# First two halves' plain output tiles moved ahead of both pairs; half of the third half's transposes given to transfers

## Chip, cores and metric

The kernel runs on one core of one Trainium2 chip. Its time is the device time of one execution in microseconds (us); before the change the median of four runs is 237.45 us (237.02 to 237.99). The engines are named as the profile names them: PE multiplies matrices, DVE, ACT and POOL work element by element, SP only issues transfers. POOL issues transfers too (the profile's software queue; SP's are the hardware queue).

## What is computed

Attention over 4 batches of 8 heads, 768 positions of 64 values, followed by a gated feed-forward network. A query sees the first 8 keys and the last 96:

```python
scores = scale * np.matmul(q, k.transpose(0, 1, 3, 2))
keep = is_global | is_local
scores = np.where(keep, scores + bias, -1000000000.0)
a = softmax(scores)
x = np.matmul(a, v)          # then (B, H, S, D) -> (B*S, H*D) = (3072, 512)
out = (np.maximum(x @ w_gate, 0.0) * (x @ w_val)) @ w_out   # 512 -> 1536 -> 512
```

Inputs and result are float32; the chip multiplies in 16-bit types.

## The kernel before

**Tiling.** The 3072 rows are eight halves (half a sequence, 384 rows each), numbered 0 to 7; the code writes s for a half in attention and c in the network. A half has four pairs of heads p = 0 to 3 in attention, and three tiles of 128 rows in the output stage.

**Attention of a half.** Keys and queries are loaded as float32 (`load_qk`, L113) and cast to 16 bits. They must then be transposed so that the head dimension lies over the partitions. Halves 0 and 1 do it on PE. Half 2 does so too: `cast` (L826, two POOL casts a pair), then `T2_piece` (L982), which makes six PE transposes of 128x128 (`piece_t`, L299), three DVE copies that put the keys into order (`piece_copy_k`, L278 to L280) and one ACT copy of the queries (L985). Halves 3 to 7 use `early_pieces` (L378): POOL casts (`piece_cast2`, L367), six transposing transfers from SP (`piece_x`, L372), and three POOL copies a pair that put the keys into order (`piece_order`, L276, which shows as L278 to L284). Then `attention_pieces` (L543) makes scores (L515), ACT exponentials (L524), DVE masks (L536), the product with the values (`piece_av`, L431), and the division (ACT L440 and L446, DVE L453).

**Values.** `load_v_half` (L162) loads the first eight rows of a batch (POOL L141) and spreads them to the other key tiles with six small copies from SP (L146), which wait for that load; then it loads the rest (POOL L154).

**Network of a half.** For each of twelve blocks of hidden columns a gate product and a value product of four matmuls each (`products`, L748). ACT makes the rectified gate (L757), DVE multiplies it with the value product into `ht` (L764). All of these go through three PSUM banks, `ff_ps`: a product can start only when an earlier bank's reader is done. Weights come in three groups of four blocks, `wg` and `wv` 0 to 2 (L173), cast in flight on POOL's queue.

**Output stage.** A plain tile (`single`, L791) is four parts of three 512-column matmuls (L781), an ACT copy (L786) and a store from SP (L787). Two tiles together (`Pair`, L605) take seven products of half-size blocks rather than eight (L634), with sums of `ht` blocks made by DVE beforehand (`sums`, L627 to L630), sums of weights made once (`weight_sums`, L600), and additions afterwards (L647). Halves 0 and 1 have one plain tile and one pair each; later halves pair up their third tiles too.

**Order.** Every engine runs its instructions in the order in which they are written. The head of the kernel is written out by hand (L838 to L981). From there `weave` (L813) interleaves: a list of network items sets the pace, each with the same weight, and attention pieces are placed at fractions of that list. The first weave (L988) has 20 items, the second (L994) 38: the last blocks of halves 0 and 1, and then their output stages, while attention of half 2 and the preparation of half 3 go in between. `F0[8]` to `F0[11]` are gate 4, value 4, gate 5 and value 5 of half 0.

Of the kernel before, what the change touches and what calls it, by code (L numbers as in the profile page):

```python
# [10 lines left out]
FP16 = mybir.dt.float16  # L11
# [5 lines left out]
def kernel(  # L17
# [12 lines left out]
    nc = tc.nc  # L30

    B, H, S, D = q.shape
# [6 lines left out]
    HP = H // 2  # L39
    QH = S // 2  # L40
    NN = 3
# [13 lines left out]
    for half in range(2):  # L55
# [32 lines left out]
    qTb = [const.tile([128, HP, 2, QH], BF16, name=f"qT{i}") for i in range(2)]  # L88
    kNb = [const.tile([128, HP, QH], BF16, name=f"kN{i}") for i in range(2)]

    qT2 = [qTb[1].rearrange("d p e t -> d (p e t)")[:, i * HP * QH : (i + 1) * HP * QH].rearrange(
        "d (p t) -> d p t", p=HP) for i in range(2)]
    qc = [const.tile([128, NN, DM], BF16, name=f"qc{i}") for i in range(2)]
    kc = [const.tile([128, NN, DM], BF16, name=f"kc{i}") for i in range(2)]
# [11 lines left out]
    def w_of(t, dc, fc):  # L106
        f = fc % GW
        return t[fc // GW][:, dc, f * 128 : (f + 1) * 128]


    qs_of, ks_of = {}, {}

    def load_qk(s, h0, h1, eng=nc.sync):  # L113
        b, half = divmod(s, 2)
        if s not in qs_of:
            qs_of[s] = stage.tile([128, H, NN * D], FP32, name="qs")
            ks_of[s] = stage.tile([128, H, NN * D], FP32, name="ks")
        for src, dst in ((k, ks_of[s]), (q, qs_of[s])):
            eng.dma_start(
                out=dst[:, h0:h1, :],  # L120
                in_=src[b, h0:h1, half * QH : (half + 1) * QH, :].rearrange(
                    "h (p n) d -> p h (n d)", n=NN))
# [17 lines left out]
    def load_v_globals(b):  # L140
        nc.gpsimd.dma_start(out=v_dst(b, 0, NG, 0),  # L141
                            in_=v[b, :, 0:NG, :].rearrange("h p d -> p h d"))
# [19 lines left out]
    def load_v_half(s):  # L162
        b, half = divmod(s, 2)
        if half == 0:
            load_v_globals(b)
            spread_v_globals(b)
        for j in range(4) if half == 0 else range(4, NT):
            load_v(b, j)
# [4 lines left out]
    def load_w_group(i):  # L173
        load_w(wg[i], moe_w_gate, i * GW * 128, (i + 1) * GW * 128)
        load_w(wv[i], moe_w_val, i * GW * 128, (i + 1) * GW * 128)
# [190 lines left out]
    def piece_cast2(s, p, dst, src):  # L366
        nc.gpsimd.tensor_copy(  # L367
            dst[s % 2].rearrange("t n (h d) -> t h n d", d=D)[:, 2 * p : 2 * p + 2],
            src[s][:, 2 * p : 2 * p + 2, :].rearrange("t e (n d) -> t e n d", n=NN))

    def piece_x(dst, src, n):
        nc.sync.dma_start_transpose(out=dst[:, :, n * 128 : (n + 1) * 128], in_=src[:, n])  # L372

    def piece_order(s, p):
        b, half = divmod(s, 2)
        put_keys(nc.gpsimd.tensor_copy, nc.gpsimd.tensor_copy, kT[b % 2][p], kNb[s % 2][:, p], half)
# [209 lines left out]
    NP = N_FC // 2  # L586
# [151 lines left out]
    def ffn_pieces(c):  # L738
        ht_of[c] = ht = ht_pool.tile([128, N_FC, QH], FP16, name="ht")
        st = {}  # L740
        pair = Pair((c, 0), (c, 1))
        first = {}

        def products(key, w, fc, d0, d1):
            if d0 == 0:
                st[key] = ff_psum.tile([128, 512], FP32, name="ff_ps")
            for dc in range(d0, d1):
                nc.tensor.matmul(st[key][:, 0:QH], lhsT=w_of(w, dc, fc), rhs=xT_of[c][:, dc, :],  # L748
                                 start=(dc == 0), stop=(dc == N_DC - 1))
            return st[key]  # L750

        def gate(fc, d0=0, d1=N_DC):
            psg = products(f"g{fc % 4}", wg, fc, d0, d1)
            if d1 < N_DC:
                return
            gr = gr_pool.tile([128, QH], BF16, name="grelu")
            nc.scalar.activation(gr, psg[:, 0:QH], AF.Relu, bias=0.0, scale=1.0)  # L757
            st["r", fc] = gr

        def val(fc, d0=0, d1=N_DC):  # L760
            psv = products("v", wv, fc, d0, d1)
            if d1 < N_DC:
                return
            nc.vector.tensor_tensor(ht[:, fc, :], psv[:, 0:QH], st["r", fc], op=ALU.mult)  # L764

            if c > 1 and 7 <= fc < N_FC - 1:
                if fc == 7:
                    first[0] = pair.sums(0, 4)
                first[0][fc - 7]()

        f1 = []
        for fc in range(N_FC):
            f1.append((0.65, lambda *d, fc=fc: gate(fc, *d)))
            f1.append((0.65, lambda *d, fc=fc: val(fc, *d)))

        def outp(n, part, after):
            if part == 0:
                st["o"] = ff_psum.tile([128, DM], FP32, name="ff_ps")
            ps2 = st["o"]
            for fc in range(part * NP // 2, (part + 1) * NP // 2):  # L780
                nc.tensor.matmul(ps2, lhsT=ht[:, fc, n * 128 : (n + 1) * 128], rhs=wo_sb[:, fc, :],  # L781
                                 start=(fc == 0), stop=(fc == N_FC - 1))
            if part == 3:
                osb = obuf[:, n_results[0] % 2, 0:2]
                n_results[0] += 1
                nc.scalar.copy(osb, ps2)  # L786
                nc.sync.dma_start(out=out_v[c, n], in_=osb)  # L787
            for f in after:
                f()

        def single(n, *after):  # L791
            after = after or ((),) * 4
            return [(0.65, lambda part=part: outp(n, part, after[part])) for part in range(4)]

        late = pair.sums(0 if c < 2 else 4, NP)
        if c < 2:
            return f1, single(2, *([f] for f in late)) + pair.items()
        if c % 2 == 0:
            return f1, pair.items({"1": late[0:2], "2": late[2:4]}, fresh=True)

        space = qTb[0].rearrange("d p e t -> d (p e t)").bitcast(FP16)
        across = Pair((c - 1, 2), (c, 2), space.rearrange("t (s c z) -> t s c z", s=4, c=NP))
        sums = across.sums(0, NP)
        return f1, (pair.items({"1": late[0:2], "2": late[2:4], "4": sums[0:1], "6": sums[1:2], "5": sums[2:4]}, fresh=True)
                    + across.items(split=c == NHALF - 1))


    def spread(items, first, last, n=None):

        n = n or len(items)  # L810
        return [(first + (i + 0.5) / n * (last - first), f) for i, (_, f) in enumerate(items)]

    def weave(f_items, *placed):  # L813
        total = sum(t for t, _ in f_items)
        a_items = sorted((x for p in placed for x in p), key=lambda x: x[0])
        done, ai = 0.0, 0
        for t, f in f_items:
            f()
            done += t
            while ai < len(a_items) and a_items[ai][0] * total <= done:  # L820
                a_items[ai][1]()
                ai += 1
        for _, f in a_items[ai:]:
            f()
# [3 lines left out]
        piece_cast(s, p, 0, eq)  # L828

    V, P, A = nc.vector, nc.gpsimd, nc.scalar  # L830
    f1_0, f2_0 = ffn_pieces(0)
    f1_1, f2_1 = ffn_pieces(1)
    G = [slice(2 * GW * i, 2 * GW * (i + 1)) for i in range(N_FC // GW)]
    F0 = [f for _, f in f1_0]
    LAST = N_DC - 1
# [85 lines left out]
    piece_biased(1, 0)  # L921
    load_v(0, 3, 24)
    load_w_group(1)
    load_w_group(2)
    load_qk(2, 0, H, nc.gpsimd)
    load_w(wo_sb, moe_w_out, 0, DM)
    for f in gate[0:3]:
        f(0, LAST)
# [35 lines left out]
    piece_inverse_wide(1, 2)  # L964
    piece_ln_wide(1, 3)
    piece_mul_wide(1, 2)
    F0[9]()
    piece_inverse_wide(1, 3)
    piece_mul_wide(1, 3)
    F0[10]()  # L970
    F0[11]()
    for p in range(HP):
        nc.gpsimd.memset(kT[1][p][:, 3, 32:128].bitcast(mybir.dt.uint32), 0)
# [1 line left out]
    nc.gpsimd.memset(vbuf[1][:, NT - 1, :].bitcast(mybir.dt.uint32), 0)  # L975
    for j in range(NT):
        fill_ones(nc.gpsimd, 1, j)
    for p in range(HP):
        cast(2, p, P, P)
    load_v_half(2)  # L980

    def T2_piece(p):  # L982
        piece_t(2, p, *QKB, apart=True)
        piece_copy_k(2, p)
        nc.scalar.copy(qT2[0][:, p], tp_of[2, p, 0])  # L985

    T2 = [(0.0, lambda p=p: T2_piece(p)) for p in range(HP)]
    weave(f1_1[G[0]] + f1_0[G[1]][4:] + f1_1[G[1]],  # L988
          [(0.05 + 0.06 * j, lambda j=j: fill_ones(nc.vector, 0, j)) for j in range(NT)],
          [(0.1 + 0.2 * i, lambda h=h: setup_mask(h)) for i, h in enumerate((0, 1, 6, 7))],  # L990
          [(0.6, lambda: load_qk(3, 0, H)), (0.6, lambda: load_v_half(3))],
          spread(T2, 0.55, 0.95))
    sums_wo = [(0.0, f) for i in (0, 3) for f in weight_sums(i, i + 3)]
    weave(f1_0[G[2]] + f1_1[G[2]] + f2_0 + f2_1,  # L994
          spread(attention_pieces(2), 0.02, 0.86, 30), spread(early_pieces(3), 0.1, 0.76),
          spread(sums_wo, 0.08, 0.4))

    for c in range(2, NHALF):
        placed = []
# [6 lines left out]
        f1, f2 = ffn_pieces(c)  # L1006
# [36 lines left out]
```

The softmax here doesn't subtract the row's maximum and nothing guards it: scores larger than these inputs give would overflow.

## Time and profile before

| what | value |
|---|---|
| median of four runs | 237.45 us |
| the profiled execution: its time | 237.38 us |
| its span, first to last instruction | 235.6 us |
| outside the span | 1.8 us |
| PE busy | 97% of the span |
| DVE, ACT, POOL busy | 79%, 62%, 38% |
| granted TensorE clock | 0.999 |
| read from and written to memory | 28.38 and 6.29 MB |

The chain of work that ended last lies 79% on PE, 7% on POOL, 6% on DVE and 4% on transfers. A row of a timeline gives start, duration, engine, line, operation, what is written and read, and a count; square brackets give the idle time of the engine before it and what ended it. PE durations overlap: what a group costs is the distance from its start to the start of the next. In `ff_ps<-xT,wg` the tile left of the arrow is written.

### The profile page before, as it was taken

The page shows a single profiled execution, that of the slowest core. Times are in us where ns is not written, and L with a number is a line of the kernel's source. Part 1 is how long each engine was busy: PE and PEld are TensorE (multiplying, and loading weights), DVE is VectorE, ACT ScalarE, POOL GpSimd, SP SyncE. Part 2 cuts the span into 40 slices and gives each one's busy share as a digit, 9 for nine tenths or more (in the row PEclk, how much of TensorE's full clock was granted, in tenths as well). Part 3 has the DMA queues.
Part 4 walks back from the last instruction along what each step waited for, and adds up shares of the span by engine and source line. Part 5 has one row for each costly group of instructions (what it writes and reads, how often), then busy time and mean ns, then how long its engine had stood idle before and what let it go on. Part 6 is the DMA issues. An engine that isn't in the chain of part 4 may idle for free.

```text
span 235.6 us, 5509 instructions
## 1 busy us (share of the span) xinstructions
PE 229.2 (97%) x2021; PEld 158.2 (67%) x2021; DVE 186.5 (79%) x466; ACT 146.0 (62%) x321; POOL 89.0 (38%) x191
## 2 busy tenths in 40 slices
PE   8889999999999999999999999999999999999994
PEld 4675756655778666856688666856679566865683
DVE  6878767779988779786999789886899779773784
ACT  7999855677624887467742887567842687524300
POOL 8998904933492066406580066306230000000000
PEclk9999999999999999999999999999999999999999
DMA  6999999998369856856497854857512200020005
GB/s 169 207 174 182 205 273 271 173 108 266 70 168 163 266 145 95 52 180 201 90 81 120 253 159 90 53 151 228 91 24 89 92 0 3 0 92 0 1 3 178
DMA packets 71419, 30.43 MB, mean 129 GB/s; under 512 B 47744, under 2 KB 70784, under 8 KB 71392
## 3 DMA queue, kind: packets, MB, share of 16 engines
q0 software_dynamic: 34896, 10.27, 38.8%
q1 hardware_dynamic: 36496, 19.82, 30.1%
q8 instruction: 16, 0.26, 0.4%
q14 instruction: 11, 0.09, 0.1%
HBM read 28.38 MB, written 6.29 MB: 147 GB/s over the span
## 4 chain that ended last, share of the span: by engine, by line
PE 79%; POOL 7%; DVE 6%; DMA 4%; issue 2%; ACT 1%; POOLq 0%; DVEq 0%
PE ff_ps L748 46%; PE ff_ps L634 20%; PE av_ps L431 6%; DMA wv<-in_moe_w_val_dram 4%; POOL vbuf L154 3%; PE ff_ps L781 2%; PE av_ps L515 2%; PE qk_ps L515 1%; DVE ht L764 1%; POOL kc L131 1%; DVE wo_sum L600 1%; DVE obuf L647 1%; DVE es L536 1%; POOL wg L171 1%; ACT es L524 1%
## 5 line engine op out<-in xcount | busy, mean ns | idle before, releaser
L757 ACT ACTIVATE grelu<-ff_ps 128x384 bf16<-128x384 f32 x96 | 46.7, 489 | 52.1 <-PE ff_ps L748 39.0
L748 PE MATMUL ff_ps<-xT,wv 128*128 128x384 bf16 x384 | 78.0, 327 | 0.2 <-DMA wv<-in_moe_w_val_dram 0.2
L748 PE MATMUL ff_ps<-xT,wg 128*128 128x384 bf16 x384 | 77.8, 326 | 0.0
L764 DVE TENSOR_TENSOR ht<-ff_ps,grelu 128x384 f16<-128x384 f32 x96 | 53.4, 557 | 27.2 <-PE ff_ps L748 22.9
L748 PEld LDWEIGHTS <-wv 128*128 128x128 bf16 x384 | 36.0, 98 | 24.2 <-issue 1.3
L748 PEld LDWEIGHTS <-wg 128*128 128x128 bf16 x384 | 36.4, 97 | 21.2 <-issue 0.5
L647 DVE TENSOR_TENSOR obuf<-ff_ps,obuf 128x512 f32<-128x512 f32 (+1 forms) x46 | 27.6, 604 | 5.3 <-ACT rcp L446 2.2
L367 POOL CAST kc<-ks 128x384 bf16<-128x384 f32 x20 | 10.6, 569 | 54.0 <-DMA ks<-in_k_dram 54.0
L453 DVE TENSOR_TENSOR xT<-av_ps,rcp 64x384 bf16<-64x384 f32 x48 | 26.5, 552 | 5.1 <-ACT rcp L446 4.3
L536 DVE TENSOR_TENSOR es<-es,m_all 128x432 bf16<-128x432 bf16 (+3 forms) x108 | 30.3, 326 | 0.2 <-ACT es L524 0.2
L440 ACT ACTIVATE lnd<-av_ps 64x384 f32<-64x384 f32 x48 | 23.3, 485 | 11.1 <-PE av_ps L431 10.3
L524 ACT ACTIVATE es<-qk_ps 128x432 bf16<-128x432 f32 (+2 forms) x54 | 27.7, 532 | 0.0
L154 POOL DMA_DIRECT2D vbuf<-in_v_dram x29 | 24.7, 861 | 0.1
L431 PE MATMUL av_ps<-es,vbuf 128*128 128x216 bf16 (+4 forms) x216 | 21.4, 226 | 0.0
L431 PEld LDWEIGHTS <-vbuf 128*128 128x128 bf16 x216 | 18.2, 98 | 4.8 <-DVE xT L453 0.4
L634 PEld LDWEIGHTS <-ht 128*128 128x128 f16 x198 | 18.6, 97 | 3.4 <-DVE ht L764 0.5
L634 PEld LDWEIGHTS <-hsum 128*128 128x128 f16 x192 | 18.5, 98 | 2.1
L634 PE MATMUL ff_ps<-wo_sb,ht 128*128 128x256 f16 x132 | 18.5, 272 | 0.2 <-DVE ht L764 0.2
L634 PE MATMUL ff_ps<-wo_sum,hsum 128*128 128x256 f16 x144 | 17.2, 273 | 0.0
L446 ACT ACTIVATE rcp<-lnd 128x384 f32<-128x384 f32 x24 | 12.6, 524 | 0.7
L524 ACT ACTIVATE es<-av_ps 128x432 bf16<-128x432 f32 (+2 forms) x18 | 9.5, 528 | 2.0 <-PE qk_ps L515 2.0
L515 PEld LDWEIGHTS <-kT 64*128 64x128 bf16 x216 | 6.6, 94 | 6.1 <-issue 3.8
(130 smaller groups left out, 264.2 us busy)
## 6 DMA issues: line engine op xcount, KB each, us to landing
out_dram<-obuf SPq DMA_DIRECT2D x22, 256.0 KB
ks<-in_k_dram SPq DMA_DIRECT2D x5, 768.0 KB
qs<-in_q_dram SPq DMA_DIRECT2D x5, 768.0 KB
vbuf<-in_v_dram POOLq DMA_DIRECT2D x23, 120.0 KB, 4.6
wv<-in_moe_w_val_dram POOLq DMA_DIRECT2D x3, 512.0 KB, 9.8
wo_sb<-in_moe_w_out_dram POOLq DMA_DIRECT2D x1, 1536.0 KB, 21.1
wg<-in_moe_w_gate_dram POOLq DMA_DIRECT2D x2, 512.0 KB, 9.8
ks<-in_k_dram SPq DMA_DIRECT2D x4, 192.0 KB
```

The source lines that it names most:

```text
L154: nc.gpsimd.dma_start(out=v_dst(b, NG + r0, NG + r0 + n, j), in_=v[b, :, KT * j + r0 : KT * j + r0 + n, :].rearrange("h p d -> p h d"))
L431: nc.tensor.matmul(av3[:, :, a : a + w], lhsT=vb[:, j, z0 : z0 + 128], rhs=es[:, c : c + NN * w].rearrange("k (n p) -> k n p", n=NN), star ...
L440: nc.scalar.activation(ln[o0 : o0 + 64], av[d0 : d0 + 64, 0:QH], AF.Ln, bias=0.0, scale=1.0)
L453: nc.vector.tensor_tensor(xT_of[s][r, p, :], av_of[s, p, e][r, 0:QH], av_of[s, p, "r"][r], op=ALU.mult)
L515: nc.tensor.matmul(banks[e][:, c : c + NN * w], lhsT=kT[b % 2][p][r, j, :], rhs=q3[:, :, a : a + w], start=True, stop=True)
L524: nc.scalar.activation(es[:, 0:cols], ps[:, 0:cols], AF.Exp, bias=0.0, scale=scale)
L536: nc.vector.tensor_mul(e4, e4, mk)
L634: nc.tensor.matmul(ps[:, c0 : c0 + DH], lhsT=lhs(i), rhs=rhs(i), start=(i == 0), stop=(i == NP - 1), skip_group_check=True)
L647: add = lambda o, x, y: nc.vector.tensor_tensor(o, x, y, op=ALU.add)
L748: nc.tensor.matmul(st[key][:, 0:QH], lhsT=w_of(w, dc, fc), rhs=xT_of[c][:, dc, :], start=(dc == 0), stop=(dc == N_DC - 1))
L757: nc.scalar.activation(gr, psg[:, 0:QH], AF.Relu, bias=0.0, scale=1.0)
L764: nc.vector.tensor_tensor(ht[:, fc, :], psv[:, 0:QH], st["r", fc], op=ALU.mult)
```

## The change

Seven edits:

1. Pairs 2 and 3 of half 2 go the way of halves 3 to 7: POOL casts, six transfers that transpose 128x256 blocks (a new first pair `p` in `piece_x`), six POOL copies for the keys. Pairs 0 and 1 stay on PE; their casts come after those of pairs 2 and 3, and they are placed at 0.65 to 0.95 of the first weave.
2. Keys and queries of half 2 are loaded ahead of the third group of weights, not behind it.
3. Gate 5 of half 0 goes ahead of value 4.
4. The first weave takes the rest of half 0's second group ahead of half 1's first group.
5. The output stages of halves 0 and 1 run as plain tile, plain tile, pair, pair (before: plain tile, pair, plain tile, pair).
6. The pair of half 0 keeps its sums in the query buffer of half 0, which is free by then. Its sums are placed behind the parts of half 1's plain tile, and those of half 1's pair between products of half 0's pair.
7. The sums of weights are spread over 0.1 to 0.4 of the second weave (before: 0.08 to 0.4).

```diff
-    def piece_x(dst, src, n):
-        nc.sync.dma_start_transpose(out=dst[:, :, n * 128 : (n + 1) * 128], in_=src[:, n])
+    def piece_x(dst, src, n, p=0):
+        nc.sync.dma_start_transpose(out=dst[:, p:, n * 128 : (n + 1) * 128], in_=src[:, n, 128 * p :])
...
+        space = qTb[0].rearrange("d p e t -> d (p e t)").bitcast(FP16).rearrange("t (s c z) -> t s c z", s=4, c=NP)
+        if c == 0:
+            pair = Pair((c, 0), (c, 1), space)
         late = pair.sums(0 if c < 2 else 4, NP)
-        if c < 2:
-            return f1, single(2, *([f] for f in late)) + pair.items()
+        if c == 0:
+            return f1, single(2), late, pair
+        if c == 1:
+            return f1, single(2, *([f] for f in pair_0[0])), pair_0[1].items(
+                {"1": late[0:1], "2": late[1:2], "4": late[2:3], "6": late[3:4]}) + pair.items()
...
     load_w_group(1)
+    load_qk(2, 0, H, nc.gpsimd)
     load_w_group(2)
-    load_qk(2, 0, H, nc.gpsimd)
...
-    F0[9]()
+    F0[10]()
     piece_inverse_wide(1, 3)
     piece_mul_wide(1, 3)
-    F0[10]()
+    F0[9]()
     F0[11]()
...
-    for p in range(HP):
+    for to, src in ((kc, ks_of), (qc, qs_of)):
+        for p in (2, 3):
+            piece_cast2(2, p, to, src)
+        for n in range(NN):
+            piece_x((kNb if to is kc else qT2)[0], to[0], n, 2)
+    for p in (0, 1):
         cast(2, p, P, P)
     load_v_half(2)
+    for p in (2, 3):
+        piece_order(2, p)
...
-    T2 = [(0.0, lambda p=p: T2_piece(p)) for p in range(HP)]
-    weave(f1_1[G[0]] + f1_0[G[1]][4:] + f1_1[G[1]],
+    T2 = [(0.0, lambda p=p: T2_piece(p)) for p in range(2)]
+    weave(f1_0[G[1]][4:] + f1_1[G[0]] + f1_1[G[1]],
...
-          spread(T2, 0.55, 0.95))
+          spread(T2, 0.65, 0.95))
...
-    weave(f1_0[G[2]] + f1_1[G[2]] + f2_0 + f2_1,
+    weave(f1_0[G[2]] + f1_1[G[2]] + single_0 + single_1 + pairs_01,
...
-          spread(sums_wo, 0.08, 0.4))
+          spread(sums_wo, 0.1, 0.4))
```

More of the change, by code (lines that the diff above doesn't have):

```diff
@@ L793, in single @@
             return [(0.65, lambda part=part: outp(n, part, after[part])) for part in range(4)]
+        space = qTb[0].rearrange("d p e t -> d (p e t)").bitcast(FP16).rearrange("t (s c z) -> t s c z", s=4, c=NP)
+        if c == 0:
+            pair = Pair((c, 0), (c, 1), space)
         late = pair.sums(0 if c < 2 else 4, NP)
-        if c < 2:
-            return f1, single(2, *([f] for f in late)) + pair.items()
+        if c == 0:
[3 more added lines that the diff above has]
+                {"1": late[0:1], "2": late[1:2], "4": late[2:3], "6": late[3:4]}) + pair.items()
         if c % 2 == 0:
             return f1, pair.items({"1": late[0:2], "2": late[2:4]}, fresh=True)
-        space = qTb[0].rearrange("d p e t -> d (p e t)").bitcast(FP16)
-        across = Pair((c - 1, 2), (c, 2), space.rearrange("t (s c z) -> t s c z", s=4, c=NP))
+        across = Pair((c - 1, 2), (c, 2), space)
         sums = across.sums(0, NP)
@@ L830 @@
     V, P, A = nc.vector, nc.gpsimd, nc.scalar
-    f1_0, f2_0 = ffn_pieces(0)
-    f1_1, f2_1 = ffn_pieces(1)
+    f1_0, single_0, *pair_0 = ffn_pieces(0)
+    f1_1, single_1, pairs_01 = ffn_pieces(1)
     G = [slice(2 * GW * i, 2 * GW * (i + 1)) for i in range(N_FC // GW)]
```

## The prediction, made before the change was run

> **What bounds the kernel now.** First the page's busy times and slices:
>
> ```profile
> PE 229.2 (97%) x2021; PEld 158.2 (67%) x2021; DVE 186.5 (79%) x466; ACT 146.0 (62%) x321; POOL 89.0 (38%) x191
> PE   8889999999999999999999999999999999999994
> ```
>
> PE is the only engine that is nearly always busy, and in every slice but the ends. A high share can hide stalls, so next I read PE's own waits, all of them:
>
> ```profile
> PE ff_ps L249 <- DVE obuf L187: 1.0, 1, 1.0
> PE qk_ps L329 <- ACT lnd L485: 0.6, 1, 0.6
> PE av_ps L299 <- ACT obuf L263: 0.4, 1, 0.4
> PE ff_ps L344 <- DVE qT L315: 0.2, 1, 0.2
> PE ff_ps L748 <- DMA wv<-in_moe_w_val_dram: 0.2, 1, 0.2
> PE ff_ps L634 <- DVE ht L764: 0.2, 1, 0.2
> PE av_ps L515 <- DVE xT L453: 0.2, 1, 0.2
> ```
>
> The columns are total, times and longest. The first four lie in the first 17 us, which the change leaves alone. Only two of the rest (DMA wv, DVE xT) lie where it acts. So time is won only by taking work off PE or ending these two waits, and lost only where PE gets a new wait. PE's timeline, the DVE's and POOL's and SP's, and the transfer shares by window, say how near such waits are.
>
> **1. Pairs 2 and 3 of half 2 by transfers.** PE's timeline around the transposes:
>
> ```profile
> 39.95 0.50 PE L299 MATMUL qk_ps<-ident,obuf 128*128 128x128 bf16 x6
> 40.28 0.81 PE L748 MATMUL ff_ps<-xT,wg 128*128 128x384 bf16 x4
> 40.93 0.81 PE L748 MATMUL ff_ps<-xT,wv 128*128 128x384 bf16 x4
> 41.58 0.50 PE L299 MATMUL qk_ps<-ident,obuf 128*128 128x128 bf16 x6
> 41.92 0.81 PE L748 MATMUL ff_ps<-xT,wg 128*128 128x384 bf16 x4
> ```
>
> Six transposes take 0.33 to 0.34 us from start to next start, with no gap on either side. Two pairs go: 2 x 0.335 = **-0.67 us**. The Trainium skill says more: "TensorE: Matmul & The Clock Gate", Part 4 (PE-mode transpose), puts a 128x128 transpose in a kernel's context at about 275 ns. Twelve would be 3.3 us and the result 234.1 us. The row's own mean is 219 ns, near that figure, but the six start 56 ns apart: the figure is the length of one, not what it holds PE for. I take the row.
>
> Also removed: six DVE copies of keys (per pair 0.52 + 0.17 + 0.2 to 0.4, 2 us in all) and two ACT copies of 0.48. PE waited for neither between 30.2 and 58.9, so they count nothing; neither backlog reaches the second weave (DVE waits for PE 0.74 us at 48.06).
>
> Added: the four casts on POOL replace four of the same size. Six key copies on POOL, at half 4's rows 0.53 + 0.2 to 0.48 + 0.22 to 0.47 each pair, make 2 to 3 us. SP issues six transfers at most as long as half 3's 1.2 to 2.0 us, under 9 us on a queue that idles from 4.8 to 46.9. Queued behind them are SP's six spreads of values (L146) and the loads for half 3.
>
> The keys' timing: POOL now waits for half 2's keys and queries:
>
> ```profile
> 37.21 0.50 POOL L263 CAST obuf<-ks 128x384 bf16<-128x384 f32 x1 [7.50 <-DMA ks<-in_k_dram]
> 39.18 0.51 POOL L263 CAST obuf<-qs 128x384 bf16<-128x384 f32 x1 [1.47 <-DMA qs<-in_q_dram]
> ```
>
> The load of queries took 2.0 us behind that of keys, and wv of group 1 landed at 30.14. Loaded next, keys land near 32.1 and queries near 34.1. Casts and transfers follow; with both slowed twofold the ordered keys are there by 45. Pair 2 is first scored at 51.7: cost zero, cover 6 us. The third weights slip from about 35 to 39; first used at 46.5: zero. The output weights keep their place in the queue.
>
> What is not covered so well is the transfers' share. Half 3's six full-size transposes took, by share times window, 0.47 x 1.25, 0.52 x 1.25, 0.41 x 2.0, 0.57 x 1.1, 0.42 x 1.4 and 0.57 x 1.0, about 0.6 us each (one window holds part of a store). Half-size ones: 0.3 each, 1.8 us, laid among casting loads that keep the share at 1.2. No row shows the two kinds side by side. From below, the overlap in that share swallows them: 0. From above, each small packet costs twice: 3.6 us. "DMA: Bandwidth & Descriptors", section on queues, rings and completion order, says that each engine takes turns between queues by packet, which speaks against the change, since 256-byte-row transposes get turns beside the weights; but it loses the loads no more than the transposes' own time. By the rule 1.8 us, by the worst reading 3.6; I take 1.8 as the upper part of what is likely. It delays the output weights (landed 46.7, DVE wants them at 50.7), the values and the spreads behind them. These were all down by 51.5 (the share falls from 2.28 at 50.5 to 0.35 at 51.5). Their reader, L431, starts at 54.14, or 53.5 with PE 0.64 ahead by then (items 1 and 2): cover 2.0 us, and 0.2 more because the last key tile is read fourth. Cost taken as zero, but only just: 0 to +1.4.
>
> **2. Gate 5 ahead of value 4.** PE's timeline:
>
> ```profile
> 29.53 0.48 PE L468 MATMUL qk_ps<-kN,vbuf 128*64 128x72 bf16 x10
> 30.19 0.82 PE L748 MATMUL ff_ps<-xT,wv 128*128 128x384 bf16 x4 [0.18 <-DMA wv<-in_moe_w_val_dram]
> ```
>
> Groups of L468 lie 0.31 apart, and a change to L748 costs 0.1 (26.11 to 26.52). Without the wait the next group starts at 29.94: 0.25 us is lost here (the 0.18 is counted from a modelled end). Gate 5 has its weights, and value 4 then starts at 30.6, behind the landing at 30.14: **-0.25**.
>
> It buys a new wait. ACT now makes gate 5's relu (0.85 after the gate's start: 30.79) ahead of pair 3's inverse, which starts at 31.19 and ends at 31.71 (before: 30.57 to 31.09). DVE multiplies pair 3's xT at 31.74 and value 4's ht behind it, 32.21 to 32.77. Two values now stand side by side (value 4, value 5, gate 6, value 6), so value 6, due at 32.54, finds all three banks held: by ht 4 until 32.77, gate 6 until 33.23, value 5 until 33.24. With 0.05 for the signal it starts at 32.82: **+0.28**. From below 0, if a bank comes free sooner; from above +0.75, if it is given gate 6's bank. I take ht 4's, whose reader ends first. Half 1's gates start 2.6 us later than before in the order, so xT's delay of half a us costs nothing.
>
> **3. The sums of weights from 0.1.** DVE's timeline:
>
> ```profile
> 56.93 0.68 DVE L536 TENSOR_TENSOR es<-es,m_all 128x432 bf16<-128x432 bf16 x1
> 57.54 0.85 DVE L600 TENSOR_TENSOR wo_sum<-wo_sb,wo_sum 128x768 f16<-128x768 f16 x1
> 58.31 1.13 DVE L453 TENSOR_TENSOR xT<-av_ps,rcp 64x384 bf16<-64x384 f32 x2
> ```
>
> DVE is full from 50.4, and PE's next scores (L515) wait for the first xT. The products before end at 57.94 + 0.65, plus 0.09 for the change of form: 58.68; scores started at 58.91, 0.23 late. The seventh sum stands at 0.08 + 6.5/8 x 0.32 = 0.340 of the list, xT at 0.02 + 11.5/30 x 0.84 = 0.342: just behind. Now the sum is at 0.344, behind xT, which is freed of 0.55 to 0.85 us: **-0.23**. Late next is ht of block 10, which the two plain tiles do not want before 61.
>
> **4. Output order, sums elsewhere, first weave's order.** PE from 59.36 to 75.36 is 8 plain parts x 0.65 + 14 products x 0.655 + 6 value groups x 0.275 = 16.0: no idle time to win. The same instructions run on PE, DVE, ACT and SP in another order: 0. Two risks. Half 1's plain tile needs block 11's ht (61.0) by its last part, at about 63.3: covered. Two pairs back to back hand over banks without a plain tile between; half 3's pair and the pair across follow each other in 118.41 to 128.66 without a PE wait, so 0, bound 0 to +0.5. The first store precedes half 3's query transposes on SP, the second follows them, and its buffer is reused 2 us later than it lands: 0.
>
> **Sum.** -0.67 - 0.25 + 0.28 - 0.23 = -0.87. The profiled run took 237.38 us (span 235.6 and 1.8 around it): 236.51. The median lies 0.07 higher: **236.6 us**. All later stages are paced by PE, so the gain stays.
>
> **Rivals.**
> - *The banks take it back* (no change): value 6 waits 0.75, the pairs' hand-over 0.2: -0.67 - 0.25 - 0.23 + 0.95 = -0.2, 237.2 us. For it: three banks, two neighbouring values. Against: half 3 shows no hand-over wait. Chance 0.30.
> - *The transfers arrive late* (slower): transposes among the casting loads hold values and spreads back by more than they take, and L431 of half 2 waits at 53.5. Cover is 2.2 us, the gain 0.87; from 3.1 us of delay the change loses. At 4 us it is +1.8 - 0.87 = +0.9: 238.3 us. For it: share over 2 at 46.5 to 51.5 already. Against: the rule of turns. Chance 0.12.
> - *No bank wait at all*: -1.15, 236.3 us. Chance 0.13.
> - *The forecast*: 0.45.
>
> 0.3% (about what a measurement of this kernel can tell from no change) is 0.71 us, so faster is below 236.74. The forecast lies there with 0.85 of its weight: 0.38 + 0.13 + 0.03 = 0.54. Slower 0.12, the rest 0.34. Range 236.0 to 238.0: from just under the last rival to most of the way to the second.
>
> **What would show it.** L299 has 12 rows from obuf less on PE; value 4 no longer waits for wv; value 6 waits near 32.6 for DVE ht; L515 near 58.0 starts without a wait for xT; POOL's casts of half 2 start near 32. Wrong would be PE waits at L431 near 53.5 (transfers) or at L634 near 70 (banks).

## The result, and the profile after

The change made the kernel slower: 238.24 us median of 43 runs, beside 237.41 us of 64 runs of the kernel before. The ratio is 1.003, 95% interval [1.002, 1.0039], so +0.83 us where -0.87 was forecast. (Medians here and below are over all executions; ratios leave out slow ones, of which e12 has two in six and the others at most one.) The profiled execution took 238.37 us, with a span of 236.6. First its busy times, and then PE's waits, without three that lie in the first 17 us:

```profile
PE 228.5 (97%) x2009; PEld 157.2 (66%) x2009; DVE 187.2 (79%) x460; ACT 145.2 (61%) x319; POOL 92.6 (39%) x197
```

```profile
PE ff_ps L249 <- DVE obuf L187: 1.0, 1, 1.0
...
PE av_ps L299 <- DMA kc<-in_q_dram: 0.6, 1, 0.6
...
PE av_ps L431 <- DMA vbuf<-vbuf: 0.4, 1, 0.4
PE av_ps L299 <- DVE obuf L263: 0.2, 1, 0.2
```

PE has 12 matmuls and 0.7 us less, as forecast, and the waits at L748 for wv and at L515 for xT are gone. In their place stands one that the forecast had called covered: L431 for the spread values. (The second line is half 1's start at 20.3. It leaves PE 0.46 us behind the kernel before, at 20.91 where that stood at 20.45. In the profiles of all 14 kernels, whose code is the same up to there but for e5's fillers, PE reaches this place between 20.10 and 21.00, so this delay comes and goes; what becomes of it is told with the sum.) PE's timeline at the new wait, columns start and duration, first before, then after:

```profile
54.14 0.42 PE L431 MATMUL av_ps<-es,vbuf 128*128 128x216 bf16 x4
54.42 0.81 PE L748 MATMUL ff_ps<-xT,wg 128*128 128x384 bf16 x4
```

```profile
53.95 0.26 PE L431 MATMUL av_ps<-es,vbuf 128*128 128x216 bf16 x1
54.59 0.58 PE L431 MATMUL av_ps<-es,vbuf 128*128 128x216 bf16 x3 [0.39 <-DMA vbuf<-vbuf]
55.02 0.81 PE L748 MATMUL ff_ps<-xT,wg 128*128 128x384 bf16 x4
```

The group starts at 53.95 and the next work at 55.02: 1.07 us, where it took 0.28 before (54.14 to 54.42). The bracket says 0.39 because a wait is counted from the modelled end of the matmul ahead; the distance between starts says **0.79**. Its source stands on SP's queue, first before, then after:

```profile
46.89 4.83 SPq L146 DMA_DIRECT2D vbuf<-vbuf  x6
```

```profile
49.73 5.05 SPq L146 DMA_DIRECT2D vbuf<-vbuf  x6
```

The six spreads wait for the load of the eight rows, which lies behind the output weights on POOL's queue. Both landed later, and the spreads started 2.84 us later. The group's second matmul reads what the first spread wrote, and it is this spread that PE waits for, as the chain of work shows (start, duration):

```profile
49.73 4.72 DMA vbuf<-vbuf
54.45 0.14 issue
54.59 0.58 PE av_ps L431 x3
```

Further on, PE's timeline in the output stage of half 1's pair, first before, then after, and below it DVE's after the change:

```profile
70.22 0.42 PE L431 MATMUL av_ps<-es,vbuf 128*128 128x216 bf16 x4
70.50 0.82 PE L634 MATMUL ff_ps<-wo_sb,ht 128*128 128x256 f16 x6
71.15 0.42 PE L431 MATMUL av_ps<-es,vbuf 128*128 128x216 bf16 x4
71.43 0.81 PE L634 MATMUL ff_ps<-wo_sb,ht 128*128 128x256 f16 x6
```

```profile
70.60 0.42 PE L431 MATMUL av_ps<-es,vbuf 128*128 128x216 bf16 x4
71.13 0.82 PE L634 MATMUL ff_ps<-wo_sb,ht 128*128 128x256 f16 x6
71.78 0.42 PE L431 MATMUL av_ps<-es,vbuf 128*128 128x216 bf16 x4
72.23 0.27 PE L634 MATMUL ff_ps<-wo_sb,ht 128*128 128x256 f16 x1
```

```profile
70.39 0.69 DVE L647 TENSOR_TENSOR obuf<-ff_ps,obuf 128x512 f32<-128x512 f32 x1
71.00 0.58 DVE L630 TENSOR_TENSOR hsum<-ht,hsum 128x768 f16<-128x768 f16 x1
71.50 1.47 DVE L647 TENSOR_TENSOR obuf<-ff_ps,obuf 128x512 f32<-128x512 f32 x2
```

A group of L431 costs 0.275 when nothing follows late, as before; here 0.53 and 0.45. The first products of the second pair want banks that DVE's additions (L647) for the first pair still read, the first of them until 71.08, the second until 72.18: **0.43** in the two places. PE's list of waits doesn't show it.

Last, the tail. From the start of the last matmul to the span's end it was 3.74 us before and 4.20 after, **+0.46**, for the same stores. SP's six last issues, before and after:

```profile
229.00 4.05 SPq L656 DMA_DIRECT2D out_dram<-obuf  x6
```

```profile
229.53 4.37 SPq L656 DMA_DIRECT2D out_dram<-obuf  x6
```

One of the six takes SP longer than its usual 0.34 to 0.42: before, the second (0.68), with time to spare behind it; after, the fourth (1.01), which pushes the last two.

### The profile page after: what moved, and what is told of

The parts are those of the page before. It is cut to its first block, busy times and chain, and to the rows that moved or that the text cites. A ratio compares the mean times of both kernels' runs of the same rounds, so it can differ in the third digit from the quotient of the medians.

```text
span 236.6 us, 5488 instructions
## 1 busy us (share of the span) xinstructions
PE 228.5 (97%) x2009; PEld 157.2 (66%) x2009; DVE 187.2 (79%) x460; ACT 145.2 (61%) x319; POOL 92.6 (39%) x197
## 4 chain that ended last, share of the span: by engine, by line
PE 73%; DMA 11%; DVE 7%; POOL 6%; issue 2%; ACT 1%; POOLq 0%; DVEq 0%
PE ff_ps L748 43%; PE ff_ps L634 19%; PE av_ps L431 5%; DMA vbuf<-in_v_dram 5%; DMA kc<-in_q_dram 4%; DMA vbuf<-vbuf 2%; PE av_ps L515 2%; DVE obuf L647 1%; POOL vbuf L154 1%; PE qk_ps L515 1%; DVE xT L453 1%; DVE es L536 1%; POOL kc L131 1%; DVE wo_sum L600 1%; POOL obuf L263 1%
## 5 line engine op out<-in xcount | busy, mean ns | idle before, releaser
L748 PE MATMUL ff_ps<-xT,wv 128*128 128x384 bf16 x384 | 77.8, 327 | 0.1
L748 PE MATMUL ff_ps<-xT,wg 128*128 128x384 bf16 x384 | 77.8, 326 | 0.0
L748 PEld LDWEIGHTS <-wv 128*128 128x128 bf16 x384 | 36.0, 98 | 24.1 <-issue 1.6
L748 PEld LDWEIGHTS <-wg 128*128 128x128 bf16 x384 | 36.5, 97 | 21.6 <-issue 0.5
L367 POOL CAST kc<-ks 128x384 bf16<-128x384 f32 x22 | 11.5, 561 | 55.0 <-DMA ks<-in_k_dram 52.3
L536 DVE TENSOR_TENSOR es<-es,m_all 128x432 bf16<-128x432 bf16 (+3 forms) x108 | 31.8, 341 | 0.2 <-ACT es L524 0.2
L647 DVE TENSOR_TENSOR obuf<-ff_ps,obuf 128x512 f32<-128x512 f32 (+1 forms) x46 | 27.6, 603 | 5.2 <-ACT rcp L446 2.2
L431 PE MATMUL av_ps<-es,vbuf 128*128 128x216 bf16 (+4 forms) x216 | 21.8, 226 | 0.4 <-DMA vbuf<-vbuf 0.4
L431 PEld LDWEIGHTS <-vbuf 128*128 128x128 bf16 x216 | 18.2, 98 | 5.6 <-issue 0.7
L634 PEld LDWEIGHTS <-ht 128*128 128x128 f16 x198 | 18.7, 97 | 3.5 <-issue 0.5
L634 PE MATMUL ff_ps<-wo_sb,ht 128*128 128x256 f16 x132 | 18.4, 272 | 0.1
L634 PEld LDWEIGHTS <-hsum 128*128 128x128 f16 x168 | 16.3, 98 | 1.9
L634 PE MATMUL ff_ps<-wo_sum,hsum 128*128 128x256 f16 x126 | 14.9, 273 | 0.0
L367 POOL CAST qc<-qs 128x384 bf16<-128x384 f32 x22 | 11.5, 560 | 1.7 <-DMA qs<-in_q_dram 1.5
```

What stands on the lines that cost most here:

```text
L367: nc.gpsimd.tensor_copy(dst[s % 2].rearrange("t n (h d) -> t h n d", d=D)[:, 2 * p : 2 * p + 2], src[s][:, 2 * p : 2 * p + 2, :].rearrange ...
L431: nc.tensor.matmul(av3[:, :, a : a + w], lhsT=vb[:, j, z0 : z0 + 128], rhs=es[:, c : c + NN * w].rearrange("k (n p) -> k n p", n=NN), star ...
L536: nc.vector.tensor_mul(e4, e4, mk)
L634: nc.tensor.matmul(ps[:, c0 : c0 + DH], lhsT=lhs(i), rhs=rhs(i), start=(i == 0), stop=(i == NP - 1), skip_group_check=True)
L647: add = lambda o, x, y: nc.vector.tensor_tensor(o, x, y, op=ALU.add)
```

## The experiments

Each ran beside the kernel before on the same chip; ratios are to those runs of it. "After" is the changed kernel.

**Undoing one edit.** In e1 pairs 2 and 3 go back to PE:

```diff
-    for to, src in ((kc, ks_of), (qc, qs_of)):
-        for p in (2, 3):
-            piece_cast2(2, p, to, src)
-        for n in range(NN):
-            piece_x((kNb if to is kc else qT2)[0], to[0], n, 2)
-    for p in (0, 1):
+    for p in range(HP):
         cast(2, p, P, P)
     load_v_half(2)
-    for p in (2, 3):
-        piece_order(2, p)
...
-    T2 = [(0.0, lambda p=p: T2_piece(p)) for p in range(2)]
+    T2 = [(0.0, lambda p=p: T2_piece(p)) for p in range(HP)]
...
-          spread(T2, 0.65, 0.95))
+          spread(T2, 0.55, 0.95))
```

> The changed kernel with only its first edit undone: all four pairs of half 2 are transposed on PE again, every other edit stays. My theory: the transfers delay the output weights by 2.9 us and with them the value spreads, and PE waits 0.8 us for these at L431 near 54; without them that wait is gone, PE has 0.67 us more transposes, and the median is 238.24 - 0.8 + 0.67 = 238.1. Rival (the loss lies in the head before 20 us and in the tail, which the first edit doesn't reach): 238.24 + 0.67 = 238.9, and the wait at L431 is there or not without bearing on the sum.

Measured: 237.37 us, ratio 1.0002 [0.9988, 1.0017], below what either expected. The spreads start at 47.72 and L431's group takes 0.39. So of the 2.84 us by which they were late, 2.0 came with the transfers; 0.83 is there without them, and its source was not separated. (One trace each: in the four other kernels with the transfers and the spreads in their old place, e2, e5, e8 and e10, the spreads start between 49.26 and 49.89.) The tail is 3.74 and the two hand-overs lose 0.13: neither belongs to the transfers by any path that was thought of, which led to e5.

In e2 edits 5 and 6 are undone:

```diff
-        if c == 0:
-            return f1, single(2), late, pair
...
+        if c < 2:
+            return f1, single(2, *([f] for f in late)) + pair.items()
...
-    weave(f1_0[G[2]] + f1_1[G[2]] + single_0 + single_1 + pairs_01,
+    weave(f1_0[G[2]] + f1_1[G[2]] + f2_0 + f2_1,
```

> The changed kernel with its output stages of halves 0 and 1 in the order of before (plain tile, pair, plain tile, pair; sums as before), all else as changed. My theory: two pairs back to back make PE wait twice for banks, 0.26 and 0.18 us near 71 and 72, behind additions and sums on DVE; those waits go, the one at L431 near 54 stays: 238.24 - 0.43 = 237.8. Rival (head and tail): 238.2, no difference.

Measured: 238.31 us, ratio 1.004 [1.0024, 1.0056]: a miss. The trace has no late product near 71, but its tail is 4.54, with one store's issue of 1.33 us. The theory's 0.4 was won at 71, and 0.34 of it lost at the end against the changed kernel's trace; the medians show no gain at all.

In e3 the load of the eight rows goes ahead of the output weights; e4 is e2 and e3 together:

```diff
+    load_v_globals(1)
     load_w(wo_sb, moe_w_out, 0, DM)
...
-    load_v_half(2)
+    spread_v_globals(1)
+    for j in range(4):
+        load_v(1, j)
```

> The changed kernel with one load moved: the first eight value rows of batch 1 are loaded ahead of the output weights and not behind them; the spreads stay behind the transposing transfers on SP. My theory: the spreads then start near 41 us and not at 49.7, PE's wait of 0.8 us at L431 near 54 is gone, and the median is 238.24 - 0.8 = 237.45, even with the kernel before. Rival (head and tail): 238.2.

> The changed kernel with the output order of before and the first value rows loaded ahead of the output weights. My theory: both waits are gone, 238.24 - 0.43 - 0.8 = 237.0, faster than the kernel before by 0.4; PE keeps only the bank wait of 0.26 at value 6 of half 0 near 33. Rival (head and tail): 238.2.

Measured: 241.77 us, ratio 1.0187 [1.0161, 1.0214], and 241.63 us, 1.0191 [1.0161, 1.022]. Both miss by 4 us, for a reason of their own. POOL's timeline of e3:

```profile
40.25 2.01 POOL L159 MEMSET vbuf<- 128x288 uint32 x7 [12.25 <-DMA vbuf<-in_v_dram]
```

The ones written beside the values now stood behind that load, and with them all of half 2's casts, for 12.25 us; PE stood 2.7 us for these at L299. L431 did take only 0.39, but later. The next experiment mends the order.

**The tail.** e5 puts 24 PE instructions more into the warm-up, so that PE runs as many as before:

```diff
-        for _ in range(n):
+        for _ in range(n - 2):
             nc.tensor.matmul(wps, lhsT=warm, rhs=warm.unsqueeze(1).to_broadcast([128, 4, 128]), start=True, stop=True)
+        for _ in range(14):
+            nc.tensor.matmul(wps[:, 0:16], lhsT=warm, rhs=warm[:, 0:16], start=True, stop=True)
```

> The changed kernel with 24 more PE instructions ahead of everything else (in the warm-up, five full and fourteen 16-column matmuls in place of seven full ones; they feed nothing), so that PE runs about as many instructions as before the change. Theory: the slow store among the last six is SP giving an issue while PE fetches its next 256 instructions (a 16 KB packet of the instruction queue); with the old count the last fetch falls back to about 229 us, the slow store is no longer among the last four, the stretch from the last matmul to the span's end is 3.7 to 3.8 us rather than 4.2, and the median is 238.2 - 0.5 = 237.7 us. Rival (the tail is chance, or does not depend on the count): tail 4.2 or scattered, median 238.2.

Measured: 237.64 us, ratio 1.0012 [0.9996, 1.0028], tail 3.85: as the theory had it. PE's last matmul starts at 232.39 in its trace and in the changed kernel's, so what this trace wins lies behind it. The trace's instruction queue 8 carries 16 packets of 16 KB, spread over the span, one for about 250 of PE's 4042 matmuls and weight loads. "Runtime: NRT & Kernel Launch", section on instruction fetch mechanics, of the Trainium skill says the same of the fetch (blocks of 16 KiB, 256 instructions) and calls it mostly hidden; here it is hidden or not by where it falls. The transfer view of the changed kernel between 230.6 and 232 us, and of e5 between 229 and 230.6, has the last of these (packets, MB, share of the 16 engines in the window):

```profile
q8 instruction: 1, 0.02, 5.7%
```

```profile
q8 instruction: 1, 0.02, 3.7%
```

The slow issue moves with it: fourth of six in after, second in e5. Over all 14 profiles: in the seven with the old count the last packet comes with or ahead of the second store, and the tail is 3.5 to 3.85. In six of the seven with 24 instructions fewer it comes just ahead of the fourth store, which takes 1.0 to 1.5 us to issue, and the tail is 4.2 to 4.7. The seventh, e12, has such a packet and no slow store (tail 3.7). In the other 13 the slow issue, second or fourth, ends 0.37 to 0.41 us after the packet does, about its usual length: as if it could only start when the packet was through. So the count sets the place of the risk; that the fetch itself holds the issue back is likely by this, but e12 speaks against an issue always being held, and no run shows how it would come about.

**The values' first rows.** e6 is e3 mended: the ones are written before the load.

```diff
+    nc.gpsimd.memset(vbuf[1][:, NT - 1, :].bitcast(mybir.dt.uint32), 0)
+    for j in range(NT):
+        fill_ones(nc.gpsimd, 1, j)
+    load_v_globals(1)
     load_w(wo_sb, moe_w_out, 0, DM)
```

> The changed kernel with the load of half 2's first eight value rows put ahead of the load of the output weights on POOL, and the memory that it writes zeroed and given its ones before that, so that nothing on POOL waits for the load. Theory: L431 of half 2 waits because the spreads of those rows start only when their load has landed at 49.6, behind the output weights that the transfers hold back; now the spreads start near 41, the 0.79 us at 53.9 is gone, and the median is 238.2 - 0.8 = 237.4 us. Rival (the wait at L431 has another source, or is slack that is made up later): the median stays at 238.2.

Measured: 241.28 us, ratio 1.0131 [1.0093, 1.0169]. POOL no longer waited, the spreads started at 41.2, and it was still 4 us off, in the wrong direction. PE's waits, SP's timeline and the busy times by window (last three columns: granted clock, DMA share, GB/s) of e6:

```profile
PE av_ps L431 <- DMA vbuf<-in_v_dram: 3.5, 1, 3.5
```

```profile
47.26 0.40 SPq L119 DMA_DIRECT2D ks<-in_k_dram  x1
```

```profile
57.00:59.00 2.00, 1.29 (x6) 0.62 (x7) 0.00 (x0) 0.49 (x1) 1.13 (x3) 0.51 1.28 206
59.00:61.00 2.00, 2.00 (x12) 1.16 (x11) 0.42 (x1) 1.06 (x3) 1.64 (x4) 0.64 0.92 115
```

L431 now waits for the rest of the values. Half 3's keys and queries, which in the changed kernel SP issued at 54.91 behind the spreads, left at 47.26 and moved abreast of them. The spreads, waiting on SP, had kept half 3's 1.5 MB away. The stall then cost more than itself: the granted clock was 0.51 and 0.64 in the four us from 57 on.

e7 is e6 with e2's order and e5's fillers:

> e6 (values' first rows ahead of the output weights) together with the output stage and its sums in the order of before (edits 5 and 6 undone) and with e5's 24 fillers. Theory: the forecast's own sum without the three costs that it did not have (L431 0.79, hand-over of banks 0.43, last stores 0.47): -0.67 - 0.25 - 0.23 + 0.26 = -0.9 against before, 236.5 to 236.7 us, and no PE wait at L431 near 54 nor at L634 near 71. Rival (the costs come back elsewhere): 237.4 or more.

Measured: 243.29 us, ratio 1.0238 [1.0219, 1.0257]: the same collision, three waits at L431 of 5.4 us in all (the line has moved by two there), clock 0.985 over the span. It couldn't tell anything of the sum.

**The transfers alone**, on the kernel before (edits 1 and 2 of the change, nothing else):

> The kernel before with edits 1 and 2 alone (transfers for pairs 2 and 3 of half 2, keys and queries loaded ahead of the third weights). Theory: -0.67 for the twelve transposes, +0.8 for L431 of half 2 near 54, +0.5 for the last stores (24 PE instructions fewer): about +0.6 against before, 238.0 us. Rival (the forecast's term, the transfers are hidden): -0.67, 236.7 us.

Measured: 238.49 us, ratio 1.0037 [1.0022, 1.0051]. The theory's +0.6 stands, rather +0.9; the forecast's -0.67 does not. L431 waits 0.8 for the spreads in PE's list, the tail is 4.54.

**Half 3's loads behind the values.** e9 is e7, e11 is e6 with the fillers and e12 is the changed kernel, each with

```diff
-          [(0.6, lambda: load_qk(3, 0, H)), (0.6, lambda: load_v_half(3))],
+          [(0.6, lambda: load_v_half(3)), (0.6, lambda: load_qk(3, 0, H, nc.gpsimd))],
```

e10 is e5 with e2's order, without that edit.

> e7 (values' first rows ahead of the output weights, output order of before, fillers) with half 3's loads of keys and queries issued by POOL behind the values of half 2 and 3, rather than by SP. Theory: in e6 and e7 the spreads of the first rows came early and so stopped holding SP until 54.8; half 3's loads then left SP at 47 and took the values' bandwidth, and L431 waited for the values. Behind the values on one queue they cannot: no PE wait at L431 near 54, none at L634 near 71, tail 3.75, and the median is the forecast's sum, 237.5 - 0.9 = 236.6 us. Rival (the values are late because they run behind the output weights, whoever else loads): the L431 wait stays near 3 us, 240 us or more.

Measured: 236.40 us, ratio 0.9949 [0.9933, 0.9964], no wait at L431 and a tail of 3.48. This is faster than both kernels, and 0.2 us under the forecast's own figure. PE's timeline of e9 where the changed kernel lost time:

```profile
54.39 0.54 PE L433 MATMUL av_ps<-es,vbuf 128*128 128x216 bf16 x4
54.78 0.48 PE L750 MATMUL ff_ps<-xT,wg 128*128 128x384 bf16 x2
...
70.36 0.42 PE L433 MATMUL av_ps<-es,vbuf 128*128 128x216 bf16 x4
70.64 0.81 PE L636 MATMUL ff_ps<-wo_sb,ht 128*128 128x256 f16 x6
71.29 0.42 PE L433 MATMUL av_ps<-es,vbuf 128*128 128x216 bf16 x4
71.57 0.81 PE L636 MATMUL ff_ps<-wo_sb,ht 128*128 128x256 f16 x6
```

0.39 rather than 1.07, and 0.28 twice rather than 0.53 and 0.45.

> The changed kernel with e5's 24 fillers and with edits 5 and 6 undone (output stage and sums as before). Theory: against e5 (237.64) the hand-over of banks between the two pairs, 0.43, is gone and nothing else changes: 237.2 us. In e2 the same gain was hidden by a slower late store. Rival (the output order costs nothing): 237.6 us.

Measured: 237.87 us, ratio 1.0018 [1.0004, 1.0031]: no gain over e5, a miss. The trace has no late product near 71 (0.27 each), but L431 waits more (53.40 to 54.82), and near 66 PE is 0.29 late in the first pair, behind DVE. (This execution, 237.43, is one of e10's shorter ones, and e5's, 238.00, one of its longer: the two traces show where time goes, not why the medians agree.) DVE's timeline, masks and sums, first of e10, then before:

```profile
62.13 0.68 DVE L538 TENSOR_TENSOR es<-es,m_all 128x432 bf16<-128x432 bf16 x1
62.73 0.85 DVE L630 TENSOR_TENSOR hsum<-hsum,ht 128x768 f16<-128x768 f16 x1
```

```profile
61.66 0.37 DVE L536 TENSOR_TENSOR es<-es,m_all 128x432 bf16<-128x432 bf16 x1
61.96 0.55 DVE L628 TENSOR_TENSOR hsum<-hsum,ht 128x768 f16<-128x768 f16 x1
```

The same two instructions took 0.68 and 0.85 rather than 0.37 and 0.55. POOL was done with half 3's casts at 61.3 before; in e10 it casts until 63.9, since half 3's loads leave SP only behind the late spreads. So the late spreads also cost DVE time where the output order was to give it back.

> e9 with the changed output order kept (edits 5 and 6 not undone), that is e6 with half 3's loads behind the values on POOL and with the fillers. Theory: 237.64 (e5) less the 0.79 at L431: 236.9 us; against e9 the hand-over costs 0.3 to 0.4. Rival on L431: 240 us or more. Rival on the order: as e9.

Measured: 236.86 us, ratio 0.9966 [0.9953, 0.9978]: as the theory said. Against e5 only the two moves that free L431 differ: -0.8 by the medians, -1.1 by the ratios. Against e9 only the output order: +0.46 by the medians, +0.4 by the ratios, and 0.38 in the trace at the two places (0.52 and 0.41 rather than 0.28).

> A control: the changed kernel with nothing but half 3's loads moved from SP to POOL behind the values. Theory: the spreads of half 2 still start only after the output weights, so L431 still waits about 0.8 and the median stays at 238.2. Rival (half 3's loads by themselves are what delays L431, or POOL's place for them gains something): below 237.6.

Measured: 242.36 us, ratio 1.0145 [1.0096, 1.0193]. The rival is out, since nothing was gained, but the theory missed by 3 us or more. PE's waits of e12, and the chain that ends the last of them:

```profile
PE av_ps L431 <- DMA vbuf<-vbuf: 2.9, 3, 2.3
```

```profile
52.28 4.83 DMA vbuf<-vbuf
57.12 0.14 issue
57.25 0.17 PE av_ps L431
```

Here the spreads still start late (50.6), and half 3's loads left POOL at 51.3, abreast of them: the third spread landed only at 57.12. The profiled execution, 239.75, is one of the two shortest. The four others took 241.85 to 243.82, and their granted clock over the span was 0.991 to 0.983, against 0.997: most likely the clock fell behind the stall in them, as it did in e6. e9 and e11 won because both moves were made: spreads early, and half 3's loads behind the values.

## Why the prediction was wrong, by its own steps

- **Twelve transposes, -0.67:** right. PE has 12 matmuls and 0.7 us less; the row (56 ns apart), not the page's 275 ns, was the price.
- **Value 4's wait for wv, -0.25:** right; value 4 starts at 31.06, one group behind gate 5, without a wait. (PE was 0.46 late there. In e1, where it was 0.09 early, there is no wait either: gate 5 at 29.86, value 4 at 30.52.)
- **Value 6's wait for a bank, +0.28:** right, 0.26 (gate 6 at 32.36, value 6 at 33.27 rather than 33.01).
- **L515's wait for xT, -0.23:** right; scores start at 59.28, the products before end at 58.54 + 0.65 + 0.09.
- **"Cost taken as zero, but only just: 0 to +1.4":** this step failed, with 0.79. The mechanism was the second rival's, and the reader was named; sizes of terms were off. The six half-size transposes were put at 1.8 us of transfer time, from 0.3 each. The transfer view of the changed kernel between 32 and 49.7 us, where this queue carries nothing else (packets, MB, share):

```profile
q1 hardware_dynamic: 1728, 0.39, 17.9%
```

  17.9% of 17.7 us are 3.2 us, 0.53 for each, near the worst reading's 3.6. The delay that came with them was less, 2.0 us by e1, which agrees with the rule of turns between queues as the prediction used it: the loads lost no more than the transposes' own time. But 0.83 came without the transposes, for which the forecast had no term. And the cover was read too large. "These were all down by 51.5" doesn't hold: by the landings in the trace of before, the third spread, the last that this group reads, was down at 52.13 and the sixth at 52.91. The first was down at 50.53, 3.64 us after its issue; in the changed kernel it was issued 2.84 later, took 4.72 and so landed 3.92 later. A cover so close to the delay deserved more than a chance of 0.12. That the rival's 238.3 is what was measured is luck all the same: it had all of its loss at L431.

  Nor is 0.79 a fixed price. L431's wait ends with the spreads, whenever PE arrives: the next work starts at 55.02 in the changed kernel and in e5, at 54.82 in e8 and e10 and at 54.70 in e2, though PE came to L431 anywhere between 53.34 (e8) and 54.09 (e5). As long as the wait stands, whatever is gained ahead of it (0.67, 0.25) only makes it longer.
- **Banks between two pairs, "0, bound 0 to +0.5":** failed, 0.43. Half 3's pair and the pair across were the wrong row to lean on: there DVE's additions were not late. The e9 and e11 pair shows it in the chip's time, 0.4 to 0.5.
- **The tail:** not in the forecast. Counting PE instructions removed as pure gain missed that their number decides which store meets the last packet of the instruction queue: +0.46.

The sum. -0.87 + 0.79 + 0.43 + 0.46 = +0.81 stands beside +0.83 measured, but that it comes so close is luck: the terms are of two single executions, the measured figure is of medians that are good to some 0.3 us, and 0.79 depends on when PE arrived. The two traces themselves can be followed step by step, as the time by which PE is behind the kernel before:

| place | PE behind by |
|---|---|
| half 1's start, 20.91 | +0.46 (comes and goes) |
| first group of L431, 53.95 | -0.19 (transposes, value 4, value 6) |
| the work behind it, 55.02 | +0.60 |
| scores, 59.28 | +0.37 (L515) |
| end of the output stage, 76.16 | +0.80 (banks) |
| last matmul, 232.39 | +0.52 |
| end of the span | +0.99 (tail) |

Between 76.16 and the last matmul PE gains some 0.3, since the kernel before lost 0.35 near 172.8 to a product that waited for `ht` (the L634 line of its waits), which the change doesn't touch. So at 55.02 the forecast's gains were gone, and the delay at 20.91 with them: with or without it, the spreads set that time.

The three losses are taken away in turn by e5, e11 and e9: -0.6, -0.8 and -0.46 by the medians, -0.4, -1.1 and -0.4 by the ratios. e9 ends at 236.40.

## What to carry to other kernels

A transfer that is added in front of a tight load has to be costed at the last reader of the whole queue behind it, and its cover compared with the delay's upper end; a reader that is then late swallows every gain ahead of it. Before a load or a copy is freed from a wait, look at what that wait was holding back on the same queue: here half 3's 1.5 MB, which cost 3 to 5 us as soon as they could leave early. And where two such moves each lose alone (e6, e12), they can still win together (e9, e11).

## What the runs showed of the hardware that was not expected

- The clock after a stall. In e3 PE stood for 2.72 us at L299. Its timeline, and the windows around its return (third column from the end: granted clock):

```profile
44.57 0.95 PE L299 MATMUL qk_ps<-ident,obuf 128*128 128x128 bf16 x6 [2.72 <-POOL obuf L263]
```

```profile
43.00:44.00 1.00, 0.00 (x0) 0.00 (x0) 0.00 (x0) 0.00 (x0) 1.00 (x3) 1.00 1.24 208
45.00:46.00 1.00, 1.00 (x7) 0.64 (x7) 0.82 (x3) 0.39 (x1) 1.00 (x3) 0.50 0.58 112
```

  In e6 the clock fell at 57.05, 2.8 us into the stall of 3.45, and in e7 at 57.90, after a stall of 2.46, one matmul and 1.4 us more. e12's stalls, the longest 2.3 us, left the clock of its profiled execution at 1.00 in that stage. "TensorE: Matmul & The Clock Gate", Part 1, of the Trainium skill puts the point at some 3.4 us of idling; here 2.8 us were enough (e3, e6). The clock stayed at 0.50 for 3.41 us in e3 and e6 and for 6.83 in e7.
- An issue by SP and the packets of instruction queue 8: in 13 of 14 profiles one of the last stores took SP 0.5 to 1.5 us rather than 0.34 to 0.42, and ended 0.37 to 0.41 after such a packet.
- Transposing transfers among casting loads: issued within 3.9 us from 33.56, the keys' three had landed only at 43.6 (in the changed kernel).
- DVE's masks took 0.68 rather than 0.37 beside POOL's casts (e10 and before), so the time at which POOL gets its data is a cost on DVE.
